# All second parts of the expert weights subtracted on VectorE, none on GpSimd

## The chip, the cores and the metric

The kernel runs on one core of one Trainium2 chip. The metric is device time in microseconds (us) of one execution. The core has five engines that run their own queues in order and wait for each other by semaphores: PE (matmul), ACT (ScalarE), DVE (VectorE), POOL (GpSimd) and SP, which issues most transfers. POOL issues the indirect ones (gather and scatter of rows).

## The reference

Chunked attention with memory keys, then two mixture-of-experts layers over 1536 tokens of 512 features. Each layer routes every token to one of 8 experts by the largest logit, and an expert is two matrix products with a ReLU between:

```python
for e in range(E):
    mask = expert_idx == e
    h = np.maximum(x[mask] @ w1[e], 0.0)          # w1[e]: 512 x 1024
    out[mask] = gate_w[mask, None] * (h @ w2[e])  # w2[e]: 1024 x 512
```

The second layer does the same, with a capacity of 384 tokens for an expert.

## The kernel before, in words

Attention comes first (until some 75 us), then routing and the experts of layer 0, routing again, and the experts of layer 1. In the profiled execution 7 experts of layer 0 have tokens to compute and 8 of layer 1, 15 in all.

Products of an expert are done in three matmuls, so that the cheaper number format keeps the precision: every operand is split into a first part, which is the value rounded by a cast, and a second part, which is the value minus the first. A product adds first x first, first x second and second x first (lines 818 to 820, or 878 to 880).

*Weights.* Each expert has two halves, `w1` and `w2`, of 2 MB each. A half lands in one of three buffers (`raw`), loaded by SP in four transfers (lines 183 and 188). It is split in eight pieces of 128 x 512: `split` has ACT cast the piece into `whi` (line 756), and then another engine subtract, `wlo = raw - whi` (line 757). There is one pair `whi0`, `wlo0` for `w1` and one pair `whi1`, `wlo1` for `w2`.

*First phase* of expert e, `first`: eight products of `w1` on PE. Each waits for nothing but its bank and its pieces. Behind each, ACT takes the ReLU into the first part of the activations (`hx0`, line 834) and VectorE the second part (`hx1`, line 835), and one piece of `w2` of the same expert is split. There are four banks `mm` in turn, so a product writes the bank that was last used four products earlier. The matmuls are 224, 320 or 384 tokens wide, chosen at run time by `tc.If`.

*Between the phases*, `columns` transposes the gathered rows of the next expert on PE, and ACT and VectorE split them into `xs0` and `xs1` (lines 807, 808).

*Second phase*: the product with `w2`. In layer 0 `second_columns` has four products of 24 matmuls, and two pieces of the next expert's `w1` are split behind each. In layer 1 `second_rows` has up to three blocks of rows, with three, three and two pieces split behind them, and ACT scales the result into `yr` (line 894).

*Which engine subtracts*: `pieces(i, j, pool, done)` gives the pieces in order; those whose number is in `pool` go to GpSimd, the others to VectorE. In the first phase that is 3, 5 and 7 of `w2`, in the second 2 and 5 of the next `w1`. Instructions stand on each engine in the order in which the program gives them; there is no reordering by a planner.

*Queues around it.* At the beginning of each expert GpSimd issues the gather of the next expert's rows (line 793) and the scatter of the last one's (line 932); both stand in GpSimd's queue with its subtractions. SP loads the next half into a buffer once both the casts and the subtractions that read it are done.

Of the kernel before, what the change touches and what calls it, by code (L numbers as in the profile page):

```python
# [15 lines left out]
ALU = mybir.AluOpType  # L16
# [16 lines left out]
def kernel(  # L33
# [15 lines left out]
    nc = tc.nc  # L49
# [145 lines left out]
    def fr(ap):  # L195
        return ap.bitcast(F32R)
# [310 lines left out]
    EARLY = (KF, 6)  # L507
# [221 lines left out]
    def load_upto(m):  # L729
        while loaded[0] <= min(m, 4 * E - 1):  # L730
            for _ in load_half(loaded[0]):
                pass
            loaded[0] += 1
# [3 lines left out]
    def parts(i, j, n):  # L737

        c = KD if j == 0 else KF
        if j == 0:  # L740
            sl = (slice(None), slice(None), slice(n * P, n * P + P))
        else:
            sl = (slice(None), slice(n % 2 * (KF // 2), n % 2 * (KF // 2) + KF // 2), slice(n // 2 * P, n // 2 * P + P))
        return [t.rearrange("p (c f) -> p c f", c=c)[sl] for t in (w_raw[i, j], whi[j], wlo[j])]

    def pieces(i, j, pool=(), done=0):

        if i < 2 * E:
            for n in range(PIECES):
                yield parts(i, j, n), nc.gpsimd if n in pool else nc.vector, n >= done  # L750

    def split(p):
        if p is not None:
            (w, h, l), eng, hi = p
            if hi:
                nc.scalar.copy(fr(h), w)  # L756
            eng.tensor_tensor(fr(l), w, h, op=ALU.subtract)  # L757

    def weights():
        v = [("p (c f) -> p c f", dict(c=KD)), ("p (c d) -> p c d", dict(c=KF))]  # L760
# [4 lines left out]
    def next_bank():  # L765
        return mm[next(turn_of) % 4]
# [13 lines left out]
    def layer_run(layer, src, r):  # L780
# [10 lines left out]
        def gather(e):  # L791
            for a in range(NA):
                nc.gpsimd.indirect_dma_start(  # L793
                    xrow[e % 2][:, a, 0:src.shape[1]], None, src,
                    bass.IndirectOffsetOnAxis(ap=idx[:, e * NA + a:e * NA + a + 1], axis=0),
                    bounds_check=N - 1, oob_is_err=False)
# [28 lines left out]
        def first(e, prep):  # L825

            w1 = weights()[0]
            hs = {}
            for f in range(KF + 1):
                if f < KF:  # L830
                    hs[f] = product(ns[e], w1, slice(f * P, (f + 1) * P), xs, KD)
                g = f - 1
                if g >= 0:
                    nc.scalar.activation(fr(hx[0][:, g, :]), hs[g], AF.Relu)  # L834
                    nc.vector.scalar_tensor_tensor(fr(hx[1][:, g, :]), hs.pop(g), 0.0, hx[0][:, g, :],  # L835
                                                   op0=ALU.max, op1=ALU.subtract)
                    if layer == 0 and e == E - 2 and 3 <= g < 3 + NA:
                        late_place(e, g - 3)
                split(next(prep, None))
# [58 lines left out]
        def late_place(e, a):  # L898

            j = (e - E + 2) * NA + a  # L900
            nc.vector.tensor_scalar(hsum[a][:, P:P + T], iota_i[:, 0:T], slot_t[:, j:j + 1], None, op0=ALU.is_equal)

        def late_logits(e):

            for a in range(NA):
                j = (e - E + 2) * NA + a
                nc.vector.tensor_tensor(hsum[a][:, 0:G * E].rearrange("p (g e) -> p g e", e=E),
                                        yrs[e % 2][:, a, DM:XW].unsqueeze(1).to_broadcast([P, G, E]),
                                        slot_g[:, j, :].unsqueeze(2).to_broadcast([P, G, E]), op=ALU.mult)
            late_sum()  # L910
# [19 lines left out]
        def scatter(e, blocks=range(NA)):  # L930
            for a in blocks:
                i_ = nc.gpsimd.indirect_dma_start(  # L932
                    dst, bass.IndirectOffsetOnAxis(ap=idx[:, e * NA + a:e * NA + a + 1], axis=0),
                    yrs[e % 2][:, a, 0:sw], None, bounds_check=N - 1, oob_is_err=False)
                scat.append(i_)
                if len(scat) > 1:
                    tc.declare_no_dep(i_.ins, group=f"scat{layer}", reason="slots hold distinct tokens")
                tc.add_to_no_dep_group(f"scat{layer}", i_.ins)
# [10 lines left out]
        for e in range(E):  # L949
            i = layer * E + e  # L950
            if e == 0 and layer == 1:
                r["gates"](None)
                r["spread_gates"]()
            if layer == 0 and e < E - 2:
                for a in range(2 * e, 2 * e + 2):
                    nc.sync.dma_start(out[a * P:(a + 1) * P, :], zero)
            if 0 < e < E - 1:
                gather(e + 1)
            if e > 0:
                scatter(e - 1)  # L960
            prep = pieces(i, 1, (3, 5, 7), EARLY[layer] if e == 0 else 0)
            if layer == 0 and e == E - 1:


                late_logits(e - 1)
                with tc.If(tail):
                    with tc.If(some):
                        first(e, prep)
                        for a in range(NA):
                            late_place(e, a)  # L970
                        second_columns(e, iter(()))
                        late_logits(e)
                        scatter(e)
                    with tc.If(more):
                        rest_run(layer, src, dst, r)
                        load_lg2()
                return
            first(e, prep)
            if e == 0:
                r["slot_gates"](next_bank())  # L980
                if layer == 0:
                    slots()
            if layer == 0 and e == E - 2:
                load_lg2()
            if e + 1 < E:
                columns(e + 1)
            prep = pieces(i + 1, 0, (2, 5))
            if layer == 0:
                second_columns(e, prep)
            else:  # L990
                second_rows(e, prep)
            for p in prep:
                split(p)
            if layer == 1 or e < E - 1:
                load_upto(2 * i + 5 if layer == 1 or e < E - 2 else 2 * E + 1)
            if e == 4:
                more = nc.values_load(r["more_i"][0:1, 0:1], min_val=0, max_val=1)

                last = nc.values_load(arms[0:1, E // 4 - 1:E // 4], min_val=0, max_val=16 ** 4 - 1) >> 12
                some = last > 0  # L1000
                tail = last + more > 0
# [3 lines left out]
    def load_lg2():  # L1005
        nc.sync.dma_start(lg2, x2_dram.rearrange("(g t) x -> t g x", t=T)[:, :, DM:XW])
# [24 lines left out]
    r1["gates"](rs1)  # L1031
    split_first(0, range(3, 8))
    layer_run(0, x_dram, r1)
    split_first(E, range(3), 0)
    r2 = route_tokens(1, lg2)
# [59 lines left out]
```

## Time and profile before

| what | value |
|---|---|
| runs | 552.27, 557.62, 552.94 us; median 552.94 |
| profiled execution | 552.76 us |
| its span, first to last instruction | 550.9 us |
| PE busy | 504.0 us (91%) |
| ACT busy | 307.0 us (56%) |
| VectorE busy | 293.8 us (53%) |
| GpSimd busy | 240.0 us (44%) |
| mean granted clock of PE | 0.964 of full speed |

A row of a group names the line of the program, the engine, the operation, what it writes and reads, and how often; then the time busy, the mean of one in ns, and the idle time just before. A row of the timeline begins with the start and the duration in us; several like instructions in a row are merged (x2, x4), and a bracket gives the idle time before and what ended it. PEld is PE's load of weights into the array, which runs ahead of the matmul.

### The profile page before, as it was taken

To read this page: it belongs to the slowest core of one execution; us is meant where nothing else is said; L and a number is where in the kernel's file an instruction comes from. 1 tells how busy PE (TensorE), PEld (TensorE's weight loads), DVE (VectorE), ACT (ScalarE), POOL (GpSimd) and SP (SyncE) were. 2 spreads that over 40 slices of the span, in tenths; PEclk is the share of its full clock that TensorE was granted. 3 is DMA by queue.
4 is the path that set the end of the run, shared out by engine and by line. 5 is a ranking of instruction groups with operands and counts; after the bars stand their busy time and mean duration, and the time that the engine had idled before them with its cause. 6 is when DMAs were issued, how large, how long until landed. Compare 5 with 4: busy or idle time off the path is not lost. (4 is left out here: it accounts for less than half of the span.)

```text
span 550.9 us, 11567 instructions
## 1 busy us (share of the span) xinstructions
PE 504.0 (91%) x3970; PEld 460.4 (84%) x3971; DVE 293.8 (53%) x735; ACT 307.0 (56%) x654; POOL 240.0 (44%) x242
## 2 busy tenths in 40 slices
PE   8899988899999999899999469899999998899991
PEld 5688856899999999899999439788889897798980
DVE  4576766634335255554436288874736284757320
ACT  6576774355445365655556374865646375655430
POOL 3042528253332445444353266665534446564230
PEclk9899988899999999999999878999999999989996
DMA  8899955742482265756465518867454637450000
GB/s 260 245 326 318 262 209 154 264 147 106 157 275 80 96 240 178 248 180 208 156 203 161 182 38 312 272 235 241 175 193 153 215 117 265 155 185 21 27 6 21
DMA packets 47574, 100.35 MB, mean 182 GB/s; under 512 B 11364, under 2 KB 12900, under 8 KB 47472
## 3 DMA queue, kind: packets, MB, share of 16 engines
q1 hardware_dynamic: 40000, 86.19, 46.7%
q0 software_dynamic: 7440, 12.71, 7.1%
q8 instruction: 74, 1.21, 0.9%
q14 instruction: 28, 0.23, 0.1%
q10 hardware_dynamic: 32, 0.02, 0.0%
HBM read 92.53 MB, written 18.22 MB: 201 GB/s over the span
## 5 line engine op out<-in xcount | busy, mean ns | idle before, releaser
L757 DVE TENSOR_TENSOR wlo<-raw,whi 128x512 fp32r<-128x512 f32 x159 | 129.5, 834 | 93.4 <-ACT whi L756 89.0
L757 POOL TENSOR_TENSOR wlo<-raw,whi 128x512 fp32r<-128x512 f32 x73 | 100.8, 1386 | 158.6 <-ACT whi L756 155.2
L818 PE MATMUL mm<-xs,whi 128*128 128x224 f32 (+2 forms) x480 | 144.2, 300 | 10.9 <-ACT whi L756 3.4
L820 PE MATMUL mm<-xs,wlo 128*128 128x224 f32 (+2 forms) x480 | 142.4, 297 | 1.9 <-issue 1.9
L819 PE MATMUL mm<-xs,whi 128*128 128x224 f32 (+2 forms) x480 | 142.3, 297 | 1.0 <-issue 1.0
L756 ACT CAST whi<-raw 128x512 fp32r<-128x512 f32 x218 | 128.1, 624 | 0.0
L818 PEld LDWEIGHTS mm<-xs,whi 128*128 128x128 f32 x480 | 94.0, 196 | 15.0 <-issue 6.7
L835 DVE SCALAR_TENSOR_TENSOR hx<-mm,hx 128x384 fp32r<-128x384 f32 x120 | 66.8, 557 | 72.9 <-ACT hx L834 66.2
L834 ACT ACTIVATE hx<-mm 128x384 fp32r<-128x384 f32 x120 | 59.3, 494 | 79.9 <-PE mm L820 76.1
L820 PEld LDWEIGHTS mm<-xs,wlo 128*128 128x128 f32 x480 | 94.0, 196 | 2.3 <-issue 2.3
L819 PEld LDWEIGHTS mm<-xs,whi 128*128 128x128 f32 x480 | 94.2, 196 | 1.3 <-issue 1.2
L818 PE MATMUL mm<-hx,whi 128*128 128x224 f32 (+2 forms) x224 | 67.2, 300 | 0.1
L820 PE MATMUL mm<-hx,wlo 128*128 128x224 f32 (+2 forms) x224 | 66.6, 297 | 0.0
L819 PE MATMUL mm<-hx,whi 128*128 128x224 f32 (+2 forms) x224 | 66.5, 297 | 0.0
L793 POOL DMA_INDIRECT xrow<-x_dram,idx x48 | 56.8, 1182 | 15.4 <-issue 10.5
L878 PE MATMUL mm<-whi,hx 128*128 128x512 f32 x128 | 51.2, 400 | 0.6 <-ACT hx L834 0.6
L880 PE MATMUL mm<-whi,hx 128*128 128x512 f32 x128 | 50.5, 394 | 0.0
L879 PE MATMUL mm<-wlo,hx 128*128 128x512 f32 x128 | 50.5, 394 | 0.0
L894 ACT ACTIVATE yr<-mm,sgate 128x512 f32<-128x512 f32 x24 | 16.0, 688 | 51.7 <-PE mm L880 51.7
L818 PEld LDWEIGHTS mm<-hx,whi 128*128 128x128 f32 x224 | 42.6, 190 | 0.3 <-issue 0.3
L819 PEld LDWEIGHTS mm<-hx,whi 128*128 128x128 f32 x224 | 42.6, 190 | 0.0
L820 PEld LDWEIGHTS mm<-hx,wlo 128*128 128x128 f32 x224 | 42.6, 190 | 0.0
(175 smaller groups left out, 656.2 us busy)
## 6 DMA issues: line engine op xcount, KB each, us to landing
raw<-in_moe_w_dram SPq DMA_DIRECT2D x128, 512.0 KB
v<-in_v_dram SPq DMA_DIRECT2D x24, 195.0 KB
kw<-in_k_dram SPq DMA_DIRECT2D x6, 576.0 KB
x_dram<-xr SPq DMA_DIRECT2D x12, 256.0 KB
out_dram<-zero SPq DMA_DIRECT2D x12, 256.0 KB
qt<-in_q_dram SPq DMA_DIRECT2D x6, 384.0 KB
kw<-in_k_dram SPq DMA_DIRECT2D x6, 192.0 KB
qt<-in_q_dram SPq DMA_DIRECT2D x6, 128.0 KB
```

The costliest lines, as they stand in the source:

```text
L756: nc.scalar.copy(fr(h), w)
L757: eng.tensor_tensor(fr(l), w, h, op=ALU.subtract)
L793: nc.gpsimd.indirect_dma_start(xrow[e % 2][:, a, 0:src.shape[1]], None, src, bass.IndirectOffsetOnAxis(ap=idx[:, e * NA + a:e * NA + a + 1 ...
L818: nc.tensor.matmul(ps[:, 0:L], fr(wh[:, k, cols]), xh, start=(k == 0), stop=False)
L819: nc.tensor.matmul(ps[:, 0:L], fr(wh[:, k, cols]), xl, start=False, stop=False)
L820: nc.tensor.matmul(ps[:, 0:L], fr(wl[:, k, cols]), xh, start=False, stop=(k == nk - 1))
L834: nc.scalar.activation(fr(hx[0][:, g, :]), hs[g], AF.Relu)
L835: nc.vector.scalar_tensor_tensor(fr(hx[1][:, g, :]), hs.pop(g), 0.0, hx[0][:, g, :], op0=ALU.max, op1=ALU.subtract)
L878: nc.tensor.matmul(ps, fr(hh), fr(wh), start=(f == 0), stop=False)
L879: nc.tensor.matmul(ps, fr(hh), fr(wl), start=False, stop=False)
L880: nc.tensor.matmul(ps, fr(hl), fr(wh), start=False, stop=(f == KF - 1))
L894: nc.scalar.activation(yrs[e % 2][:, a, 0:DM], pvs[a], AF.Copy, scale=sgate[:, e * NA + a:e * NA + a + 1])
```

## The change

`pieces` loses its argument `pool` and no longer gives an engine with a piece; `split` always subtracts on VectorE. The casts on ACT, the order of the pieces and everything else stay.

```diff
-    def pieces(i, j, pool=(), done=0):
+    def pieces(i, j, done=0):
         if i < 2 * E:
             for n in range(PIECES):
-                yield parts(i, j, n), nc.gpsimd if n in pool else nc.vector, n >= done
+                yield parts(i, j, n), n >= done
     def split(p):
         if p is not None:
-            (w, h, l), eng, hi = p
+            (w, h, l), hi = p
             if hi:
                 nc.scalar.copy(fr(h), w)
-            eng.tensor_tensor(fr(l), w, h, op=ALU.subtract)
+            nc.vector.tensor_tensor(fr(l), w, h, op=ALU.subtract)
...
-            prep = pieces(i, 1, (3, 5, 7), EARLY[layer] if e == 0 else 0)
+            prep = pieces(i, 1, EARLY[layer] if e == 0 else 0)
...
-            prep = pieces(i + 1, 0, (2, 5))
+            prep = pieces(i + 1, 0)
```

On VectorE, the end of the first phase of expert 1 in layer 1 (`wlo_1501` is the second part of `w2`, `hx_70` the second part of the activations, `mm` the banks, `xs_68` the next expert's rows) stands before as:

```order
L835 SCALAR_TENSOR_TENSOR hx_70<-mm_1493,hx_69 128x384
L757 TENSOR_TENSOR wlo_1501<-raw_1_8397,whi_1500 128x4x128
L775 UNCONDITIONAL_BRANCH
L835 SCALAR_TENSOR_TENSOR hx_70<-mm_1494,hx_69 128x384
L835 SCALAR_TENSOR_TENSOR hx_70<-mm_1491,hx_69 128x384
L757 TENSOR_TENSOR wlo_1501<-raw_1_8397,whi_1500 128x4x128
L835 SCALAR_TENSOR_TENSOR hx_70<-mm_1492,hx_69 128x384
L835 SCALAR_TENSOR_TENSOR hx_70<-mm_1493,hx_69 128x384
L808 TENSOR_TENSOR xs_68<-mm_1494,xs_67 128x4x128
```

The same place on VectorE in the changed kernel:

```order
L835 SCALAR_TENSOR_TENSOR hx_70<-mm_1493,hx_69 128x384
L757 TENSOR_TENSOR wlo_1501<-raw_1_8397,whi_1500 128x4x128
L775 UNCONDITIONAL_BRANCH
L835 SCALAR_TENSOR_TENSOR hx_70<-mm_1494,hx_69 128x384
L757 TENSOR_TENSOR wlo_1501<-raw_1_8397,whi_1500 128x4x128
L835 SCALAR_TENSOR_TENSOR hx_70<-mm_1491,hx_69 128x384
L757 TENSOR_TENSOR wlo_1501<-raw_1_8397,whi_1500 128x4x128
L835 SCALAR_TENSOR_TENSOR hx_70<-mm_1492,hx_69 128x384
L757 TENSOR_TENSOR wlo_1501<-raw_1_8397,whi_1500 128x4x128
L835 SCALAR_TENSOR_TENSOR hx_70<-mm_1493,hx_69 128x384
L808 TENSOR_TENSOR xs_68<-mm_1494,xs_67 128x4x128
```

Every `hx` but the first of the phase now has a subtraction directly ahead of it, the last one too.

On GpSimd, the same expert and the phase after it (`wlo_66` is the second part of the next `w1`, `xrow` the gathered rows, `yr` the rows to scatter) stand before as:

```order
L757 TENSOR_TENSOR wlo_1501<-raw_1_8397,whi_1500 128x4x128
L775 UNCONDITIONAL_BRANCH x2
L757 TENSOR_TENSOR wlo_1501<-raw_1_8397,whi_1500 128x4x128 x2
L757 TENSOR_TENSOR wlo_66<-raw_0_8951,whi_65 128x4x128 x2
L793 DMA xrow_1497<-x_dram,idx_8340 128x520 x2
L885 UNCONDITIONAL_BRANCH x2
L775 UNCONDITIONAL_BRANCH
L793 DMA xrow_1497<-x_dram,idx_8340 128x520
L775 UNCONDITIONAL_BRANCH
L932 DMA out_dram<-yr_1507,idx_8340 1536x512
```

In the changed kernel, from the last scatter of the expert before:

```order
L932 DMA out_dram<-yr_1506,idx_8340 1536x512
L793 DMA xrow_1497<-x_dram,idx_8340 128x520
L775 UNCONDITIONAL_BRANCH
L793 DMA xrow_1497<-x_dram,idx_8340 128x520 x2
L775 UNCONDITIONAL_BRANCH x3
L885 UNCONDITIONAL_BRANCH x2
L775 UNCONDITIONAL_BRANCH x2
L932 DMA out_dram<-yr_1507,idx_8340 1536x512
```

The five subtractions are gone, and the gather stands right behind the scatter of the expert before.

## Rows read from the trace of the kernel before

**Rows 1.** Page part 1, engines: busy us, share of span, instructions.

```profile
PE 504.0 (91%) x3970; PEld 460.4 (84%) x3971; DVE 293.8 (53%) x735; ACT 307.0 (56%) x654; POOL 240.0 (44%) x242
```

**Rows 2.** Busy time by stretch: stretch, us, engines (instructions), granted clock, DMA share, GB/s.

```profile
89.00:306.00 217.00, 211.97 (x1588) 210.58 (x1588) 103.69 (x179) 115.30 (x228) 91.08 (x81) 0.99 0.53 180
329.00:540.00 211.00, 200.66 (x1250) 180.52 (x1248) 120.22 (x181) 116.78 (x225) 107.13 (x88) 0.98 0.49 169
```

**Rows 3.** Waits of PEld: waited for, us in total, times, longest us.

```profile
PEld mm L818 <- issue: 7.0, 8, 1.7
...
PEld mm L818 <- ACT whi L756: 4.2, 2, 2.3
PEld mm L818 <- DVE hx L835: 4.1, 5, 2.0
...
PEld mm L803 <- DMA xrow<-x_dram,idx: 2.6, 2, 2.4
...
PEld tp L803 <- DMA xrow<-x_dram,idx: 2.2, 2, 1.4
```

**Rows 4.** Groups by line: count, busy us, mean ns, idle before us, releasers.

```profile
L757 DVE TENSOR_TENSOR wlo<-raw,whi 128x512 fp32r<-128x512 f32 x159 | 129.5, 834 | 93.4 <-ACT whi L756 89.0 <-DMA raw<-in_moe_w_dram 2.2 <-ACT yr L859 2.2
...
L757 POOL TENSOR_TENSOR wlo<-raw,whi 128x512 fp32r<-128x512 f32 x73 | 100.8, 1386 | 158.6 <-ACT whi L756 155.2 <-DMA raw<-in_moe_w_dram 3.4
...
L1018 DVE TENSOR_TENSOR wlo<-raw,whi 128x512 fp32r<-128x512 f32 x8 | 4.9, 686 | 0.0
```

**Rows 5.** Line 757 on VectorE: ns min/median/max, first and last start.

```profile
L757 DVE TENSOR_TENSOR wlo<-raw,whi x159: 679/693/1784, 90.4 to 525.6; 128x512 fp32r<-128x512 f32 x159
```

**Rows 6.** Timeline of VectorE, first phase of expert 1, layer 1.

```profile
354.13 0.55 DVE L835 SCALAR_TENSOR_TENSOR hx<-mm,hx 128x384 fp32r<-128x384 f32 x1
354.60 0.68 DVE L757 TENSOR_TENSOR wlo<-raw,whi 128x512 fp32r<-128x512 f32 x1
355.20 0.55 DVE L835 SCALAR_TENSOR_TENSOR hx<-mm,hx 128x384 fp32r<-128x384 f32 x1
```

**Rows 7.** Timeline of PE there, two matmuls twelve apart, none idle between.

```profile
355.98 0.27 PE L818 MATMUL mm<-xs,whi 128*128 128x224 f32 x1
...
357.32 0.27 PE L818 MATMUL mm<-xs,whi 128*128 128x224 f32 x1
```

**Rows 8.** Timelines of ACT, VectorE, GpSimd, PEld, second phase of expert 0, layer 1.

```profile
345.09 3.24 ACT L756 CAST whi<-raw 128x512 fp32r<-128x512 f32 x6
...
346.10 4.69 DVE L757 TENSOR_TENSOR wlo<-raw,whi 128x512 fp32r<-128x512 f32 x4
...
346.85 3.39 POOL L757 TENSOR_TENSOR wlo<-raw,whi 128x512 fp32r<-128x512 f32 x2 [3.37 <-ACT whi L756]
...
351.52 0.19 PEld L818 LDWEIGHTS mm<-xs,whi 128*128 128x128 f32 x1 [1.89 <-ACT whi L756]
```

**Rows 9.** Timelines of VectorE and PEld around two waits put to hx.

```profile
96.42 0.56 DVE L835 SCALAR_TENSOR_TENSOR hx<-mm,hx 128x384 fp32r<-128x384 f32 x1 [0.61 <-ACT hx L834]
...
100.44 0.56 DVE L835 SCALAR_TENSOR_TENSOR hx<-mm,hx 128x384 fp32r<-128x384 f32 x1 [0.18 <-ACT hx L834]
...
101.72 0.29 PEld L818 LDWEIGHTS mm<-xs,whi 128*128 128x128 f32 x1 [2.02 <-DVE hx L835]
...
360.40 0.56 DVE L835 SCALAR_TENSOR_TENSOR hx<-mm,hx 128x384 fp32r<-128x384 f32 x1 [0.34 <-ACT hx L834]
...
360.81 0.19 PEld L818 LDWEIGHTS mm<-xs,whi 128*128 128x128 f32 x1 [1.17 <-DVE hx L835]
```

**Rows 10.** Timelines of VectorE and PEld, between the phases, layer 0.

```profile
294.41 0.56 DVE L835 SCALAR_TENSOR_TENSOR hx<-mm,hx 128x384 fp32r<-128x384 f32 x1 [0.78 <-ACT hx L834]
...
294.89 0.19 PEld L818 LDWEIGHTS mm<-hx,whi 128*128 128x128 f32 x1
```

**Rows 11.** Timelines of GpSimd and SP's queue, end of a first phase.

```profile
342.19 1.28 POOL L757 TENSOR_TENSOR wlo<-raw,whi 128x512 fp32r<-128x512 f32 x1 [3.32 <-ACT whi L756]
...
343.50 2.90 SPq L183 DMA_DIRECT2D raw<-in_moe_w_dram  x4
```

## The prediction

> **What bounds the kernel now.** I read the page's engine totals first [rows 1]: PE is busy 504.0 of 550.9 us (91%), VectorE 293.8 us (53%), GpSimd 240.0 us (44%). A share over the whole span mixes stages, so the second view is the busy time by stretch [rows 2]. It covers the two stretches in which experts run and every instruction of the change lies. In 89 to 306 us (layer 0) PE is busy 211.97 of 217.00 us at a granted clock of 0.99; in 329 to 540 us (layer 1), 200.66 of 211.00 us at 0.98. Those are nearly the upper of the clock's two levels, 2.4 GHz. So PE is idle there for only 5.0 + 10.3 = 15.4 us, and whatever the change does for VectorE or GpSimd can give back no more than that, unless PE's own work changes, and its instructions stay as they are.
>
> The third view says what ended that idle time: the waits of PE's weight loads [rows 3], which start first in every product. They name its own sequencer ("issue"; for L818 alone 7.0 us in 8 waits), ACT's first parts (`whi`, 4.2 us in 2) and VectorE's second parts of the activations (`hx`, 4.1 us in 5). None names a second part of the weights, `wlo`, from either engine. GpSimd's 73 subtractions therefore arrive in time today, and the question is whether VectorE can take them and stay in time.
>
> **What the change removes and adds.** GpSimd loses 73 subtractions of 1386 ns, 100.8 us busy; VectorE gets the same 73 beside its 159 of 834 ns [rows 4]. 73 is 15 first phases x 3 and 14 second phases x 2.
>
> The price on VectorE is not 834 ns. The spread of that line is 679 / 693 / 1784 ns (least, median, most) [rows 5]: half of them take about 693 ns, a few far more. The eight subtractions of L1018, the same tiles, run while GpSimd does none: mean 686 ns, 4.9 us busy for eight, so 0.61 us each when back to back [rows 4]. Where both engines subtract, four on VectorE take 4.69 us from 346.10, two on GpSimd 3.39 us from 346.85, and the two lie over each other [rows 8]. So each slows the other. With GpSimd out I take 232 on VectorE at 0.61 (back to back) to 0.69 us (alone): 142 to 161 us busy, against 129.5 now. VectorE's load rises by 12 to 31 us, 0.4 to 1.1 us in each of the 29 phases, not by 73 x 0.834 = 61 us.
>
> A rule of the Trainium skill says what this row shows: SBUF — State Buffer, section "Who interferes with whom", has VectorE's second SBUF input and a GpSimd instruction that reads SBUF share an interface, and the later one waits. The trace agrees (median 693, most 1784 ns). By the rule VectorE's 159 would get back 159 x (834 - 693) = 22 us. The sum below does not use it, as that time is not PE's.
>
> **Where VectorE's extra work lies.** *First phase.* The order on VectorE was subtraction, hx, subtraction, hx, with pieces 3, 5 and 7 left out; now none is left out. One product on PE takes 1.34 us in the narrowest form, 224 tokens: four groups of three matmuls from 355.98 to 357.32 [rows 7]. Where VectorE has both to do, hx starts at 354.13 and again at 355.20 with a subtraction between: 1.07 us a pair [rows 6]. So VectorE has 0.27 us over in every product, and wider products leave more. What stands behind the waiting instruction: a subtraction waits for ACT's cast of its piece, and the hx behind it waits for ACT's ReLU, which stands behind that cast on ACT. The order is the same on both, so nothing new is held up by that wait. The only hx on which PE could wait is the last. Of layer 0, it starts at 294.41 and ends at 294.97, while PE starts the second phase at 294.89 [rows 10]; PE needs it for the last of its eight inner steps, after 21 matmuls of 1.34/12 = 0.11 us, at 297.2. That cover is 2.2 us; one moved subtraction ahead of it is 0.61 to 0.69. Cost nothing. If the cover were gone, each microsecond beyond it would be PE's in that phase.
>
> *Second phase, layer 1.* Six subtractions now follow each other on VectorE from 346.10, in place of four there and two on GpSimd. ACT's six casts end at 345.09 + 3.24 = 348.33 [rows 8], so VectorE is done at 346.10 + 6 x 0.61 = 349.8, or 350.2 at 0.69. Before, it was done at 350.79. A gain of 0.6 to 1.0 us for VectorE, hidden: the pieces are for the next expert, whose first product starts at 351.52. *Second phase, layer 0*: two subtractions (1.2 to 1.4 us) beside each of four column products of 24 matmuls x 0.11 = 2.7 us. Cost nothing.
>
> *Weight loads.* SP's next load waits for the last reader of the buffer. In layer 1's first expert that was GpSimd's piece 7, 342.19 + 1.28 = 343.47, and the load is issued at 343.50 [rows 11]. On VectorE it could end about 0.6 us earlier. The loads come a little sooner; no wait of PE in [rows 3] ends with one, so this is worth nothing.
>
> *GpSimd's queue.* Gathers of the next expert stood behind the subtractions and now follow the scatter of the expert before directly. PE's waits for gathered rows are four, 2.6 + 2.2 us [rows 3], all before the first expert of a layer, whose gathers have no subtraction ahead of them. Worth nothing.
>
> *Sum*: 0 for PE in each of the 29 phases. The profiled execution took 552.76 us (span 550.9 and 1.9 around it), 0.2 below the median 552.94 of the runs shown; 552.8 + 0 = **552.8 us**.
>
> **What is unknown, from both sides.** On the side of a gain: of the waits of [rows 3], those put to hx and whi (4.1 + 4.2 = 8.3 us) could be real waits on queues that get freer. I take 0, because the rows contradict the label. PE's wait that ends at 101.72 stands before product 7 of its phase, which writes the bank of product 3; the hx that freed that bank ran from 96.42 to 96.98, and even the last hx before the wait's end was over at 100.44 + 0.56 = 101.00. The wait that ends at 360.81 is put to an hx that runs from 360.40 to 360.96, so beyond PE's start [rows 9]. I read these as waits for PE's own instructions. On the side of a loss: the waits put to PE's own sequencer, 7.0 us for L818, could grow if the earlier loads and gathers fall on them; doubled, +7.0 us. I take 0, which is nearest to rows that tie none of them to VectorE or GpSimd, and for the range about half of each end, -4 and +4.5 us (the whole ends are A and C below).
>
> **Rivals.**
> *A, faster.* The waits put to hx and whi are real, caused by the slowed subtractions, and vanish: 552.8 - 8.3 = 544.5 us. For it: the profile's labels, and subtractions of up to 1784 ns on VectorE's queue. Against it: the two rows above. Chance 0.07.
> *B, slower, one mechanism.* VectorE becomes the pace of the first phases, because the long subtractions come from something other than GpSimd, and all of them then take 1.39 us, between the four of [rows 8] (4.69/4 = 1.17) and the longest (1.78). A pair then takes 1.07 - 0.61 + 1.39 = 1.85 us against PE's 1.34, so hx is 8 x 0.51 = 4.1 us late at the end, 1.9 beyond the cover of 2.2; 15 phases make 28 us: 581 us. It decides from a pair of 1.34 + 2.2/8 = 1.62 us on, that is a subtraction of 1.16 us. Against it: 0.61 to 0.69 for eight in a row at L1018. Chance 0.04.
> The Trainium skill (Perfetto Trace Analysis, "Optimizing Scalar/DVE Operations") allows giving work to GpSimd where VectorE is saturated, and doubts that it helps, as the two share a port. Where VectorE were saturated this change would cost time, as in B; the trace does not agree that it is: 120.22 of 211.00 us [rows 2].
> *C, slower.* The waits put to PE's own sequencer double, as loads and gathers now fall on them: 552.8 + 7.0 = 559.8 us. For it: they are the largest of the three [rows 3], and the gathers do shift. Against it: the loads move by 0.6 us only, and PE's instructions are the same. Chance 0.06.
>
> **How the numbers follow.** No change: 0.83; A 0.07; B 0.04; C 0.06. About 1% (5.5 us) is what a measurement of this kernel can tell from no change. Faster by over 1%: A, 0.07, and 0.01 of the tail of the first case: 0.08. Slower: B and C and nothing else, 0.10. Same: 0.82. Range: 552.8 - 4 to 552.8 + 4.5, so 548.8 to 557.3; A, B and nearly all of C (0.17) lie outside.
>
> **What would show it.** The subtraction line on VectorE: 232 at a mean of 0.66 to 0.70 us with no long ones; 142 to 161 us busy; GpSimd at about 139 us. PE busy in the experts' stretches within 1 us of 212 and 201, and no PE wait for `wlo`. Wrong would be: a PE wait named for `wlo` or hx that is longer than those of [rows 3] and comes again in each phase (B), or the waits put to hx and whi gone with the time down by 8 us (A), or "issue" waits well over 7.0 us (C).

## The result

The change made the kernel a little slower: 558.71 us median of 20 runs (554.65 to 566.17) against 553.86 us of 20 runs of the kernel before beside it (548.15 to 563.80), a ratio of 1.0093, 95% interval 1.0070 to 1.0117. That is just within the 1% called "no change" above, but 1.4 us over the top of the range. A ratio leaves out the runs of either kernel that took over 1.5% more than its fastest; the medians are of all runs. The profiled execution took 558.98 us, 6.2 us more than that of before.

The engine totals answer to [rows 1], the two stretches of the experts to [rows 2] (page of the changed kernel; then busy time by stretch: us, PE, PEld, DVE, ACT, POOL, granted clock, DMA share, GB/s).

```profile
PE 505.6 (91%) x3970; PEld 460.1 (83%) x3971; DVE 313.1 (56%) x808; ACT 304.5 (55%) x654; POOL 137.2 (25%) x169
```

```profile
89.00:306.00 217.00, 207.90 (x1549) 205.02 (x1548) 117.15 (x212) 112.42 (x224) 48.23 (x46) 0.99 0.53 180
329.00:540.00 211.00, 198.16 (x1241) 178.04 (x1239) 130.66 (x228) 118.83 (x234) 51.98 (x53) 0.98 0.49 170
```

The granted clock is what it was (0.99 and 0.98). PE's idle time in these two stretches rose from 15.4 us to 9.1 + 12.8 = 21.9 us, but they no longer hold the same work: layer 1's first matmul of an expert is at 335.56 us here and was at 329.35, so the second stretch begins with 6 us of routing. From the first matmul of a layer's experts to the end of their last, for the kernel before and then for the changed one:

```profile
89.17:305.87 216.70, 211.68 (x1587) 210.45 (x1587) 103.69 (x179) 115.21 (x227) 90.91 (x81) 0.99 0.53 180
329.35:539.20 209.85, 200.43 (x1248) 180.49 (x1248) 120.22 (x181) 116.01 (x224) 106.78 (x88) 0.98 0.49 170
```

```profile
90.89:310.95 220.06, 211.89 (x1586) 209.48 (x1587) 118.44 (x214) 113.71 (x227) 46.73 (x46) 0.99 0.52 177
335.56:545.51 209.95, 200.30 (x1248) 180.29 (x1248) 125.42 (x220) 114.60 (x224) 47.62 (x50) 0.98 0.48 170
```

PE is busy there as long as before. Of the 6.3 us that the span has grown by, 1.7 stand ahead of the first expert, where the change has no instruction; 3.4 are in layer 0's experts, nearly all of it idle PE; 1.1 lie between the layers; layer 1's experts add 0.1. The subtractions did what was forecast; this is their group and their spread, as in [rows 4] and [rows 5].

```profile
L757 DVE TENSOR_TENSOR wlo<-raw,whi 128x512 fp32r<-128x512 f32 x232 | 154.9, 693 | 93.9 <-ACT whi L756 82.2 <-DMA raw<-in_moe_w_dram 9.7 <-ACT yr L894 1.8
...
L757 DVE TENSOR_TENSOR wlo<-raw,whi x232: 675/685/1132, 91.7 to 533.2; 128x512 fp32r<-128x512 f32 x116
```

The waits of PE's weight loads, as in [rows 3]:

```profile
PEld mm L818 <- issue: 6.0, 6, 3.4
PEld mm L818 <- ACT yr L894: 4.4, 3, 1.7
...
PEld mm L818 <- ACT whi L756: 4.2, 2, 2.3
...
PEld mm L818 <- DVE wlo L757: 3.0, 2, 1.9
...
PEld mm L818 <- DVE hx L835: 1.7, 1, 1.7
...
PEld mm L803 <- DVE hx L835: 1.3, 2, 0.7
```

New beside [rows 3] are `yr` (4.4 us), `wlo` (3.0 us) and L803, the transposes of the next expert's rows, which now wait for hx. The first two are not the change's: in later profiles of the kernel before, before_again has `wlo` at 2.2 us, before_third has it at 2.5 us and `yr` at 4.3. The wait at L803 stands in no profile of the kernel before.

**Where it goes.** Matmul by matmul, the largest new piece among the experts is experts 3 and 4 of layer 0, the narrow ones (224 tokens): 57.01 us from the first matmul of expert 3 to that of expert 5, where the kernel before had 54.01, so 3.0 of the 3.4 us. The first phase of expert 3 in the changed kernel, on PE (end and start of two products), ACT and GpSimd, in one timeline each (start us, us, engine, line, instruction, idle before it and what ended that):

```profile
203.91 0.27 PE L820 MATMUL mm<-xs,wlo 128*128 128x224 f32 x1
204.73 0.37 PE L818 MATMUL mm<-xs,whi 128*128 128x224 f32 x1 [0.55 <-issue]
...
203.18 0.49 ACT L834 ACTIVATE hx<-mm 128x384 fp32r<-128x384 f32 x1 [1.21 <-PE mm L820]
...
204.73 0.49 ACT L834 ACTIVATE hx<-mm 128x384 fp32r<-128x384 f32 x1 [0.56 <-PE mm L820]
...
207.65 0.49 ACT L834 ACTIVATE hx<-mm 128x384 fp32r<-128x384 f32 x1 [1.92 <-PE mm L820]
...
201.42 1.40 POOL L932 DMA_INDIRECT x_dram<-yr,idx  x1 [0.30 <-issue]
203.13 1.05 POOL L793 DMA_INDIRECT xrow<-x_dram,idx  x1 [0.31 <-PE mm L820]
204.48 1.30 POOL L793 DMA_INDIRECT xrow<-x_dram,idx  x1 [0.30 <-issue]
206.09 1.24 POOL L793 DMA_INDIRECT xrow<-x_dram,idx  x1 [0.30 <-issue]
```

Product 4 ends on PE at 203.91 + 0.27 = 204.18, and its ReLU, the one at 207.65, starts 3.47 us later, though ACT idles for 1.92 us of that. ACT waits for PE's semaphore: the trace's record of PE's semaphore events, one for each product, has this one at 207.62. They are late where GpSimd issues scatters and gathers in one row. Gathers alone do not do it (the first phase of either layer's first expert has them, and no ReLU there is over 0.1 us late), and scatters alone do hardly more than before (expert 6 of layer 0: the third ReLU is 1.00 us late, before 0.97). In the kernel before, no ReLU starts more than 1.24 us behind its product (that is right behind ACT's copies of `yr`); here 26 of 120 start more than 1.3 us behind. All 26 lie in first phases that hold both. Twelve of them are in layer 1, whose experts take no longer for it (209.95 against 209.85 us); what they cost stands in experts 3 and 4, where they are later at products 4 to 7 than in any other phase. In the kernel before the gathers stood behind GpSimd's pieces, in the second phase:

```profile
214.97 1.28 POOL L757 TENSOR_TENSOR wlo<-raw,whi 128x512 fp32r<-128x512 f32 x1 [1.91 <-ACT whi L756]
216.40 1.05 POOL L793 DMA_INDIRECT xrow<-x_dram,idx  x1
```

**How it reaches PE.** The late ReLUs make hx late, and VectorE has little slack to catch up in a narrow phase. The transposes write the banks of products 4 and 5, so they wait for the hx that reads product 5, the one that starts at 209.29 and ends at 209.84 (0.68 us at 209.89). Then PE stands for 1.95 us at 221.08, put to `wlo`. The rows are that hx on VectorE, weight loads of PE, the one product branch there (L775; min/median/max ns, first and last start), and the instruction packets from 217.4 to 221.1 us (number, MB, share), all of the changed kernel:

```profile
209.29 0.55 DVE L835 SCALAR_TENSOR_TENSOR hx<-mm,hx 128x384 fp32r<-128x384 f32 x1
...
209.89 0.42 PEld L803 LDWEIGHTS mm<-ident,xrow 128*128 128x128 f32 x4 [0.68 <-DVE hx L835]
...
221.08 0.19 PEld L818 LDWEIGHTS mm<-hx,whi 128*128 128x128 f32 x1 [1.95 <-DVE wlo L757]
...
L775 PEldq COMPARE_BRANCH  x1: 3657/3657/3657, 217.4 to 217.4; - x1
...
q8 instruction: 1, 0.02, 1.5%
```

The branch starts at 217.4 and takes 3.66 us, so it ends at 221.06, within 0.05 us of the load's start: PE's sequencer was late. What it waits for is not `wlo` (skip_pieces, below) but code: in all twenty profiles the branch at this place ends 2.4 to 2.5 us behind the start of a 16 KB instruction packet, here at 218.66. In the kernel before the same branch took 2.00 us. It takes 3.38 to 3.72 us in the three profiles with late ReLUs, where the packet starts 1.0 to 1.3 us into the branch, and 1.44 to 2.38 us in the other seventeen, where it starts ahead of the branch. So two things are to be explained: why the events are late, and whether that is the loss.

### The profile page after: what moved, and what is told of

It is laid out like the page before. It is cut to its first block, busy times and chain, and to the rows that moved or that the text cites. A ratio compares the mean times of both kernels' runs of the same rounds, so it can differ in the third digit from the quotient of the medians.

```text
span 557.2 us, 11541 instructions
## 1 busy us (share of the span) xinstructions
PE 505.6 (91%) x3970; PEld 460.1 (83%) x3971; DVE 313.1 (56%) x808; ACT 304.5 (55%) x654; POOL 137.2 (25%) x169
## 5 line engine op out<-in xcount | busy, mean ns | idle before, releaser
L757 DVE TENSOR_TENSOR wlo<-raw,whi 128x512 fp32r<-128x512 f32 x232 | 154.9, 693 | 93.9 <-ACT whi L756 82.2
L818 PE MATMUL mm<-xs,whi 128*128 128x224 f32 (+2 forms) x480 | 143.1, 298 | 13.4 <-issue 4.2
L818 PEld LDWEIGHTS mm<-xs,whi 128*128 128x128 f32 x480 | 93.3, 194 | 17.2 <-issue 5.7
L818 PE MATMUL mm<-hx,whi 128*128 128x224 f32 (+2 forms) x224 | 67.3, 300 | 2.0 <-DVE wlo L757 1.8
L932 POOL DMA_INDIRECT out_dram<-yr,idx x24 | 24.4, 1016 | 156.7 <-ACT yr L894 150.6
L932 POOL DMA_INDIRECT x_dram<-yr,idx x21 | 23.4, 1116 | 153.8 <-ACT yr L859 145.2
L793 POOL DMA_INDIRECT xrow<-x_dram,idx x48 | 53.4, 1113 | 15.8 <-issue 11.4
L818 PEld LDWEIGHTS mm<-hx,whi 128*128 128x128 f32 x224 | 42.6, 190 | 2.8 <-DVE wlo L757 1.9
```

What stands on the lines that cost most here:

```text
L757: nc.vector.tensor_tensor(fr(l), w, h, op=ALU.subtract)
L793: nc.gpsimd.indirect_dma_start(xrow[e % 2][:, a, 0:src.shape[1]], None, src, bass.IndirectOffsetOnAxis(ap=idx[:, e * NA + a:e * NA + a + 1 ...
L818: nc.tensor.matmul(ps[:, 0:L], fr(wh[:, k, cols]), xh, start=(k == 0), stop=False)
L932: i_ = nc.gpsimd.indirect_dma_start(dst, bass.IndirectOffsetOnAxis(ap=idx[:, e * NA + a:e * NA + a + 1], axis=0), yrs[e % 2][:, a, 0:sw], ...
```

## The experiments

Theories: **V**, VectorE's larger load costs; **G**, the gathers' new place in the first phase costs; **P**, it is GpSimd's queue, emptied behind the scatters, wherever the gathers are; **F**, PE's waits for code fall by chance; **C** (formed after the first four), the late events belong to a chip and make the loss there. The experiments fell on five chips, called B to F, each used in one stretch of time. The chip of the first profile of either kernel is not on record; A stands for the changed kernel's, and may be one of the five. "Experts 3 and 4" is the time from the first matmul of expert 3 of layer 0 to that of expert 5; the granted clock is 1.00 there in every profile that the table lists.

| run | chip | late ReLUs | experts 3, 4 | ratio to before, 95% |
|---|---|---|---|---|
| before | not recorded | 0 | 54.01 | |
| changed | A | 26 | 57.01 | 1.0093 (1.0070 to 1.0117) |
| late_gather | B | 0 | 52.47 | 1.0032 (0.9984 to 1.0080) |
| early_gather | B | 0 | 56.11 | 1.0085 (1.0046 to 1.0125) |
| first_only | B | 0 | 52.44 | 1.0108 (1.0053 to 1.0164) |
| second_only | B | 0 | 54.64 | 1.0038 (0.9999 to 1.0076) |
| after_again | C | 27 | 57.62 | 1.0074 (1.0026 to 1.0122) |
| skip_pieces | C | 25 | 56.13 | 1.0094 (1.0042 to 1.0146) |
| first_again | C | 0 | 53.16 | 1.0042 (0.9997 to 1.0086) |
| before_again | C | 0 | 53.61 | |
| late_again | D | 0 | 52.62 | 1.0017 (0.9988 to 1.0046) |
| hold_hx | D | 0 | 52.94 | 0.9997 (0.9962 to 1.0032) |
| no_gather | D | 0 | 52.33 | 0.9886 (0.9849 to 0.9922) |
| after_third | D | 0 | 51.94 | one run, 547.28 us |
| after_fourth | E | 0 | 52.88 | 1.0029 (0.9991 to 1.0068) |
| hold_again | E | 0 | 53.56 | 1.0047 (1.0011 to 1.0083) |
| before_third | E | 0 | 52.54 | |
| hold_third | F | 0 | 53.26 | 1.0032 (0.9998 to 1.0065) |
| after_fifth | F | 0 | 53.28 | 0.9999 (0.9959 to 1.0038) |
| early_again | F | 0 | 56.12 | |

Late ReLUs are those that start more than 1.3 us behind their product, of 120. A smaller mark of the late events does not depend on the kernel: the third ReLU of expert 3 starts 0.96 to 1.00 us behind its product in before, before_again and first_again, and 0.33 or 0.34 us in each of the fourteen profiles of chips B, D, E and F. So late events are there on chip C whichever kernel runs, and the change makes them more and later.

### The gathers' place and the two parts of the change, chip B

late_gather: the changed kernel, with GpSimd held back ahead of each gather.

```
             for p in prep:
                 split(p)
+            if e < E - 2:
+                nc.gpsimd.tensor_copy(held, parts(i + 1, 0, 5)[2][0:1, 0, 0:1])
```

> The changed kernel (VectorE does all second parts), but GpSimd has to read one element of piece 5 of the next w1 before each gather from the second layer position e=2 on, so that the three gathers of an expert run in the second phase again, as they did before the change, and not right behind the three scatters in the first phase. Theory G (the loss comes from gathers that now run in the first phase and make ScalarE's ReLUs late): the ReLUs of products 2 to 7 start within 0.1 us of their product again (apart from the 0.5 us behind the scatters that the kernel before also has), and the time is that of before: ratio to before 0.997 to 1.003. Theory V (the loss comes from VectorE's load, 232 subtractions instead of 159, wherever the gathers run): the ratio stays at 1.006 to 1.012. Theory F (the loss is TensorE's waits for its own instructions at the product branches, which fall by chance): the ratio lies anywhere from 0.995 to 1.015 and the profile's TensorE waits of over 0.6 us at L775's branches, 22.6 us before and 27.9 us after in sum, go with it.

early_gather: the kernel before, with the gathers early.

```
-            if 0 < e < E - 1:
-                gather(e + 1)
             if e > 0:
                 scatter(e - 1)
+            if e < E - 2:
+                gather(e + 2)
```

> The kernel before (GpSimd keeps its five pieces per expert), but the gather of expert e+2 is issued right behind the scatter of expert e-1, ahead of GpSimd's pieces, where the changed kernel has it. VectorE's work is untouched. Theory G: ReLUs late by 1 to 3 us in products 2 to 6 as in the changed kernel, ratio to before 1.005 to 1.012; GpSimd's first piece comes some 4 us later, which its product order leaves room for. Theory V: no change, ratio 0.997 to 1.003. Theory F: anything from 0.995 to 1.015, following the sum of TensorE's branch waits.

first_only and second_only: the kernel before with one of its two lists emptied.

```
-            prep = pieces(i, 1, (3, 5, 7), EARLY[layer] if e == 0 else 0)
+            prep = pieces(i, 1, (), EARLY[layer] if e == 0 else 0)
...
-            prep = pieces(i + 1, 0, (2, 5))
+            prep = pieces(i + 1, 0, ())
```

> The first part of the change alone: pieces 3, 5 and 7 of the second weights go to VectorE, pieces 2 and 5 of the next first weights stay on GpSimd, so the gathers behind them stay in the second phase. Theory G: ratio to before 0.997 to 1.003 and no late ReLUs. Theory V: about three fifths of the whole, 1.004 to 1.008. Theory F: 0.995 to 1.015 with the branch waits.

> The second part of the change alone: pieces 2 and 5 of the next first weights go to VectorE, pieces 3, 5 and 7 of the second weights stay on GpSimd; the gathers come behind piece 7, at the end of the first phase or the start of the second. Theory G: ratio to before 0.997 to 1.004, ReLUs late at most at the last product. Theory V: about two fifths of the whole, 1.002 to 1.006. Theory F: 0.995 to 1.015 with the branch waits.

No kernel of this chip had a late ReLU, early_gather included, though its gathers stand where the changed kernel has them. The times did not sort the theories either: first_only has the highest ratio (six runs), with experts 3 and 4 at 52.44 us, below before. Theory G as first put, that gathers in the first phase make ReLUs late by themselves, fell here.

early_gather loses for another reason: 56.11 us in experts 3 and 4. Its three pieces on GpSimd come back to back behind the gathers, beside VectorE's (timelines of GpSimd, VectorE and PE's weight loads):

```profile
205.01 3.77 POOL L757 TENSOR_TENSOR wlo<-raw,whi 128x512 fp32r<-128x512 f32 x3
...
205.93 3.40 DVE L757 TENSOR_TENSOR wlo<-raw,whi 128x512 fp32r<-128x512 f32 x1
209.26 1.01 DVE L835 SCALAR_TENSOR_TENSOR hx<-mm,hx 128x384 fp32r<-128x384 f32 x2
...
209.92 0.19 PEld L818 LDWEIGHTS mm<-hx,whi 128*128 128x128 f32 x1 [1.30 <-ACT xs L807]
```

One subtraction on VectorE takes 3.40 us instead of 0.69, hx and the new xs behind it are late, and PE waits 1.30 us, put to xs. early_again, on chip F, shows the same time of the two experts. In early_gather expert 3's second phase starts those 1.30 us late, and the branch in it takes 1.44 us; so PE's being late does not by itself make that branch long.

### Load or place, chip C

after_again and before_again are the two kernels unaltered, first_again is first_only once more. skip_pieces drops the five moved subtractions from expert 2 on:

```
-            eng.tensor_tensor(fr(l), w, h, op=ALU.subtract)
+            if eng is not None:
+                eng.tensor_tensor(fr(l), w, h, op=ALU.subtract)
...
-                yield parts(i, j, n), nc.gpsimd if n in pool else nc.vector, n >= done
+                yield parts(i, j, n), (nc.vector if i < 2 else None) if n in pool else nc.vector, n >= done
```

> The changed kernel, unaltered, on the chip of this call. Its first profile had ScalarE's ReLUs 1 to 3.5 us behind their products wherever gathers ran in the first phase, because TensorE's semaphore events (one per product) were recorded up to 3.6 us late there (33 of some 70 near a scatter or gather; 9 in the profile of before; none in the four kernels run since, early_gather with its gathers in the same place among them). Theory C (a property of that chip or execution, not of the change): if this chip shows none of it, the ratio falls to 1.000 to 1.005; if it shows it in the kernel before too, the ratio stays. Theory P (a property of the changed program): the late events are there again and the ratio is 1.006 to 1.012. Theory V (VectorE's load costs, events or not): 1.006 to 1.012 without late events.

> The changed kernel, but from the third expert on the five second parts per expert that the change moves are subtracted by no engine (their values stay those of an earlier expert). VectorE has the load of before, GpSimd that of after, gathers run where the changed kernel has them. Theory V: the time of before or a little less, ratio 0.990 to 1.002. Theory G or P (the gathers' place, or GpSimd's empty queue): still 1.006 to 1.012.

> The kernel of first_only once more (only pieces 3, 5 and 7 of the second weights go to VectorE), for a narrower interval: it had 1.0108 from six runs, which no theory of the gathers' place gives, since its gathers stay in the second phase. Theory V: 1.004 to 1.011 again. If that was six runs of chance: 0.997 to 1.004.

> The kernel before, unaltered, for its profile on this chip: the late events of TensorE (9 in its first profile) are there if they belong to the chip and execution, whichever kernel runs; theory P expects at most those 9. Time 548 to 559 us.

The late events are there again in the changed kernel (27 late ReLUs), and V falls: skip_pieces has VectorE's load of before and is as slow, 1.0094. The two experts in skip_pieces and in first_again (stretch: us, PE, PEld, DVE, ACT, POOL, clock, DMA share, GB/s):

```profile
195.63:251.76 56.13, 52.77 (x459) 51.36 (x458) 26.98 (x48) 33.71 (x68) 12.96 (x12) 1.00 0.58 197
```

```profile
197.77:250.93 53.16, 51.67 (x460) 51.28 (x458) 31.75 (x54) 34.13 (x68) 18.62 (x16) 1.00 0.62 207
```

VectorE is busy for 26.98 us in the slow one and 31.75 us in the quick one. So on one chip the same two experts lose 3.0 us with gathers in the first phase and less work on VectorE. The kernel before took 53.61 us there. skip_pieces also settles the wait put to `wlo`: the long branch is there again, 3.38 us from 215.6, and this time the load behind it is put to PE's own sequencer.

```profile
219.03 0.19 PEld L819 LDWEIGHTS mm<-hx,whi 128*128 128x128 f32 x1 [1.67 <-issue]
...
L776 PEldq COMPARE_BRANCH  x1: 3377/3377/3377, 215.6 to 215.6; - x1
```

### The gathers held or left out, chip D

late_again is late_gather once more, after_third the changed kernel. hold_hx holds the gathers only until the first phase is done; no_gather leaves them out.

```
             first(e, prep)
+            if e < E - 2:
+                nc.gpsimd.tensor_copy(held, hx[0][0:1, KF - 1, 0:1])
```

```
-            if 0 < e < E - 1:
-                gather(e + 1)
```

> The kernel of late_gather once more (VectorE does all second parts, each gather held back until piece 5 of the next first weights is subtracted), for a narrower interval than 0.9984 to 1.008 and on the chip on which the changed kernel is profiled beside it. Theory G (gathers in the first phase): experts 3 and 4 of the first layer take 52.2 to 53.0 us from their first matmul to that of expert 5, against 57.0 to 57.6 in the changed kernel's profiles and 53.6 to 54.0 in those of before; ratio 0.996 to 1.004. Theory P (GpSimd's empty queue): 56 us or more there, ratio 1.005 to 1.011.

> As late_gather, but the gather is held back only until the last ReLU of the first phase is done, so it runs from the phase boundary on, beside the columns and the start of the second phase. Theory G as put so far (in the first phase it delays the ReLUs and columns): as late_gather, experts 3 and 4 in 52 to 53.5 us, ratio 0.995 to 1.004. If any gather close to columns costs: 54 to 57 us and 1.003 to 1.010.

> The changed kernel without the gathers of experts 2 to 7 of each layer (their rows stay those of experts 0 and 1), so that GpSimd has only the scatters there. Theory G: experts 3 and 4 in 52 to 53 us, no ReLU over 1.3 us behind its product, ratio 0.993 to 1.002. Theory P (GpSimd's empty queue behind the scatters is enough): 56 us or more and 1.005 to 1.011.

> The changed kernel, unaltered, for its profile on this chip: by theory G experts 3 and 4 in 56.5 to 58 us, with ReLUs 1 to 3.5 us behind their products in the first phases that hold gathers. If the late events belong to two chips only, ReLUs are on time here and the two experts take 53 to 55 us.

Here the surprise is after_third: the unaltered changed kernel, 547.28 us in its one run. The same place in its trace as above (PE, ACT and GpSimd):

```profile
203.12 0.27 PE L820 MATMUL mm<-xs,wlo 128*128 128x224 f32 x1
203.72 0.37 PE L818 MATMUL mm<-xs,whi 128*128 128x224 f32 x1 [0.32 <-issue]
...
203.43 0.49 ACT L834 ACTIVATE hx<-mm 128x384 fp32r<-128x384 f32 x1 [0.28 <-PE mm L820]
...
202.35 1.05 POOL L793 DMA_INDIRECT xrow<-x_dram,idx  x1 [0.30 <-DVE wlo L757]
203.70 1.56 POOL L793 DMA_INDIRECT xrow<-x_dram,idx  x1 [0.30 <-PE mm L820]
...
L775 PEldq COMPARE_BRANCH  x1: 1523/1523/1523, 215.4 to 215.4; - x1
```

Product 4 ends at 203.12 + 0.27 = 203.39 and its ReLU starts at 203.43, 0.04 us later, with the same gathers beside it; the branch takes 1.52 us, and nothing of PE waits for hx at L803 there. The two experts, in the changed kernel's first profile and in this one:

```profile
197.24:254.25 57.01, 53.00 (x460) 51.37 (x458) 32.68 (x58) 33.72 (x68) 13.81 (x12) 1.00 0.59 194
```

```profile
196.46:248.40 51.94, 51.56 (x459) 51.20 (x458) 32.78 (x58) 34.27 (x68) 13.87 (x12) 1.00 0.62 214
```

5.07 us apart, with one and the same program. Aligned matmul by matmul, 1.93 us of it is that branch, 0.61 + 0.31 + 0.56 + 0.31 = 1.79 us the transposes of two experts and the first load behind each, 0.54 us a wait put to PE's own sequencer inside a product, and the rest smaller gaps. no_gather's ratio can't be read: its stale rows give layer 1 other token counts, so its widths differ. Its layer 0 can: 52.33 us, no better than the others of this chip, so gathers cost nothing there where events are in time.

### The ratio on chips without late events, chips E and F

> The changed kernel, unaltered, timed in rounds on the chip of this call. Theory C (late events of TensorE belong to a chip and make the loss there; without them the change gains): with ReLUs on time the ratio is 0.988 to 1.000 and experts 3 and 4 of the first layer take 51.5 to 53 us; with ReLUs 1 to 3.5 us late the ratio is 1.006 to 1.012 and they take 56.5 to 58 us. Theory P (the change loses on every chip, and the one run of 547 us was chance): 1.005 to 1.012 with ReLUs on time.

> The kernel of hold_hx once more (gathers held until the first phase is done). Theory C with the gathers' place as what the late events cost: 0.996 to 1.004 on either kind of chip, with experts 3 and 4 in 52 to 54 us. If the place of the gathers is nothing by itself, it follows the changed kernel: 1.006 to 1.012 on a chip with late events.

> The kernel before, unaltered, for its profile on this chip: by theory C no late ReLU (beyond the 1.25 us right behind the yr copies) on a chip where the changed kernel has none, and some 8 or 9 late events near the scatters on a chip where it has 30. Time 548 to 556 us.

> The kernel of hold_hx (gathers held until the first phase is done), on another chip. If this chip has TensorE's late events: theory C with the gathers' place expects experts 3 and 4 in 52 to 54 us and a ratio of 0.998 to 1.005, at most some 12 late events at the scatters; if only the chip matters, 56 us and more and 1.006 to 1.012. On a chip without them: 52 to 54 us and 0.997 to 1.005, as it had twice.

> The changed kernel, unaltered, beside it. With late events: experts 3 and 4 in 56.5 to 58 us, ratio 1.006 to 1.012. Without: 51.5 to 53 us, ratio 0.999 to 1.007, as on the chip of after_fourth.

> The kernel of early_gather (GpSimd keeps its pieces, gathers right behind the scatters) for its profile on this chip. With late events on this chip, theory C expects its ReLUs 1 to 3 us late in the phases with gathers; without, none, and experts 3 and 4 in some 56 us as before, from GpSimd's pieces that then come late and beside VectorE's.

Neither chip has late events, and the changed kernel stands at 1.0029 (0.9991 to 1.0068) and 0.9999 (0.9959 to 1.0038) there: no change that can be measured, 555.30 and 555.43 us median against 554.11 and 554.19. So after_third's 547.28 us was a lucky single run, not a gain. Theory C has then in its favour five profiles of the changed kernel: late ReLUs in two (57.01 and 57.62 us in the two experts; ratios 1.0093 and 1.0074), none in three (51.94, 52.88, 53.28 us; 1.0029 and 0.9999 where timed). The mean difference is 57.3 - 52.7 = 4.6 us in the two experts, and of the ratios 1.0084 - 1.0014 = 0.7%, or 3.9 us. Against the kernel before the two experts lose 57.01 - 54.01 = 3.0 us in the first profiles, 57.62 - 53.61 = 4.0 on chip C and 52.88 - 52.54 = 0.3 on chip E; the kernel before is itself slower there where events are late. The loss is of the size of what late events cost there. The ratios alone would not carry this: C's interval overlaps E's.

hold_hx, hold_again and hold_third (0.9997, 1.0047, 1.0032) beat neither kernel. They never met a chip with late events, so that holding the gathers cures such a chip rests on first_again beside after_again and skip_pieces on chip C.

**Settled and open.** Shown: the load is not the cause, and the loss in experts 3 and 4 goes with the late ReLUs, which need both gathers in the first phase (first_again and before_again on chip C have none) and the chip: of the four on record on which the unaltered change was profiled, C alone has them, and A may be C or another. Against theory P speaks expert 6 of layer 0, behind whose scatters GpSimd's queue is empty: its third ReLU is 1.00 us late in the first profile and 0.98 in skip_pieces, against 0.97 before (in after_again it is 1.71, the one late ReLU without gathers). But no run on a chip with late events held the gathers and left that queue empty. That the loss of whole runs has no other part is not shown: first_again at 1.0042 can't be told from after_again at 1.0074. Theory F alone does not sort the runs: the product branches of over 0.4 us add up to 29.6 us in the changed kernel's first profile and to 31.7 us in after_fifth, at ratios of 1.0093 and 0.9999. That the chain from late ReLU to longer branch is causal is argued from the order of the rows, not shown: no run delayed a ReLU on purpose. Why the instruction packet comes later there is open. Why the events are late on these chips is open, and so is whether the others would show it at another time. What first_only's 1.0108 was stays open too; the same kernel had 1.0042 on chip C.

## Why the prediction was right and wrong

- **Price of the moved work: right.** 232 subtractions at a mean of 693 ns, 154.9 us in all, against a forecast of 142 to 161; longest 1132 ns, where [rows 5] had 1784. GpSimd is busy 137.2 us against 139. The Trainium skill's rule weighed above (SBUF — State Buffer, "Who interferes with whom") is borne out by that: with GpSimd's subtractions gone, the mean fell from 834 to 693 ns.
- **Cover on VectorE: right by itself.** Where events are in time, the first phases keep pace (after_third to after_fifth: experts 3 and 4 at 52 to 53 us) and there no transpose waits for hx. Rival B never showed. But the prediction had "the only hx on which PE could wait is the last": it left out the transposes, which need the banks of products 4 and 5, and PE waited for the hx of product 5. With late ReLUs the slack of 0.27 us in a product [rows 6, 7] is what VectorE has to catch up with, and that is too little before the transposes: the 0.68 us at L803.
- **"GpSimd's queue … Worth nothing": the step that failed.** It asked only whether the gathered rows come in time. It did not ask what the gathers' new neighbours are: three scatters and three gathers in a row, in the phase in which ACT and VectorE follow PE product by product. On chips E and F that is worth nothing that can be measured (1.0029 and 0.9999), as put. With late events, in the first profiles and on chip C, experts 3 and 4 took 3.0 and 4.0 us longer than before, and the sum was 0 for them. In the first profile 1.3 us of it is the transposes' wait for hx (0.68 and 0.63 us), which the rows show; the longer branch goes with the late events for a reason that stays open.
- **The labels of PE's waits: right.** The waits put to hx and whi were read as waits for PE's own code, and rival A fell with them: whi is 4.2 us in 2 waits as before. The new wait put to `wlo` is of the same kind, as the branch of 3.66 us ends where it ends. "No PE wait for `wlo`" was a sign that could not tell, as two profiles of the kernel before have such waits.
- **Rival C came nearest in time, 559.8 us, and not in its mechanism.** "Issue" at L818 went from 7.0 to 6.0 us rather than to 14. One wait for code did grow, from 2.00 to 3.66 us, but no gather stands beside it (the last is issued at 206.09, 11 us ahead of the branch), and whether the weight load does anything to it is open: the load that SP issues at 211.53 still moves 0.41 MB while the branch lasts.
- **PE busy within 1 us of 212 and 201: right**, 211.89 and 200.30 us from the first matmul of a layer's experts to the end of their last. In the fixed windows of [rows 2] it reads 207.90 and 198.16, because the work in them has moved.
- **The range** started from one execution of the kernel before; over 20 runs that kernel stands at 553.86 us, 1.1 above the 552.8, nearly as much as the 1.4 us that the result lies over the top. It held what code waits do in one execution and took the measured median for steadier than a chip is. It had no term for a difference between chips, though chips with and without late events stand at a mean of 1.0084 and 1.0014.

## What to carry to other kernels

When work leaves an engine with a queue in order, list what stood behind it: the DMAs that the engine issues move too, and they need a price for their new neighbours, not only for when their data lands. Before a loss of less than 1% is given a cause, run the unaltered kernel on a second chip. And where a wait of PE stands at a product's branch, look at the length of that branch before believing the engine that the wait is put to.

## What the runs showed of the hardware

- PE's semaphore events can come up to 3.5 us behind the product that makes them while GpSimd issues scatters and gathers in one row, in the first profile of the changed program and on chip C, not on D, E and F. The kernel before shows a little of it (some 8 events more than 0.15 us late in its first profile and on chip C, none on chip E).
- The product branches of PE's sequencer take 67 ns at least, 212 ns in the middle, 5223 ns at most in the changed kernel, and the long one above waits for code. The branches of over 0.4 us come to 23.9 to 32.9 us in the profiles of the two kernels. The Trainium skill (Runtime: NRT & Kernel Launch, "Instruction fetch mechanics") says that a taken branch out of the fetched window has to wait for a fetch of its target. The trace agrees at the branch above, which ends 2.4 us behind the start of an instruction packet; no run shows the window itself. Stretches differ from run to run: the time up to expert 0, which the change does not touch, from 87.9 to 91.1 us, expert 0 from 28.3 to 34.7, expert 6 of layer 0 (to the end of its second product) from 23.8 to 28.1. The changed kernel took 547 to 566 us, the kernel before 545 to 564, so a single execution can't tell 1%.
- One subtraction of VectorE took 3.40 us, five times its 0.69, beside three back to back on GpSimd (early_gather). In the kernel before, with the same pieces spread over the phase, the longest took 1.78 us [rows 5].
